# Attention with sinks, then a gated FFN on one core: scores by blocks of 128 queries in every batch, and ten uncast weight pieces instead of nine

## The chip, the core and the metric

The kernel runs on one core of one Trainium2 chip. The metric is the device time of one execution in microseconds (us), the median of several runs. The engines are called as in the profile: PE (TensorE matmul), PEld (its weight loads), DVE (VectorE), ACT (ScalarE), POOL (GpSimd) and SP (SyncE). POOL and SP issue nearly all DMAs here: POOL those that cast float32 to bfloat16 on the way, SP the uncast ones, the transposes and the stores.

## The reference

Four batches, eight heads, 768 tokens, 64 columns a head. Each query sees the first four tokens (the sinks) and the 128 tokens that end with itself. The attention's output, as 3072 tokens of 512 columns, goes through an FFN whose two halves are multiplied, and through two more matrices.

```python
keep = is_sink | in_window                       # pos < 4, or 0 <= rel < 128
a = softmax(where(keep, (q @ k.T) / 8, -1e9))    # 768 x 768 for each of 4 x 8 heads
x = (a @ v) as (3072, 512)
out = ((x @ w1) * (x @ w2)) @ w3 @ w_out         # w1, w2: 512 x 1024; w3: 1024 x 1024; w_out: 1024 x 512
```

## The kernel before

**Weights.** w3 @ w_out doesn't depend on x, so it is computed once: the *fold*. For each of the eight row blocks i of w3 (128 rows), `fold_w3` transposes its eight 128x128 pieces on PE in two groups of four ("t3", h = 0 and 1; group h needs columns 512 h to 512 h + 511) and DVE copies them to `w3t`; `fold_mm` ("fm", four pairs a row block) multiplies piece j with row block j of w_out into a PSUM tile, and ACT copies the finished row block to `w3o`. Row block i therefore needs its own row of w3 and all eight row blocks of w_out. Row blocks 0 to 3 accumulate in the ring of score tiles (`ps_sc`, two slots, two row blocks a slot), 4 to 7 in the common ring (`ps_mm`, four slots).

**How weights arrive.** `raws` lists pieces of 0.5 MB that SP loads uncast, into buffers that are needed only later (`homes`); DVE and ACT cast them (line 418, `cast`). The other rows of w3, and w1 and w2 in four column quarters ("w12"), come through POOL's queue, in the order of `order`, between the loads of q, k and v ("qkv", batch, first and last block of 128 tokens). POOL's queue begins only when the raw piece number `hold` has landed: line 204 reads one of its columns. On SP, eight small loads of the sinks' rows of v (`vc`) stand behind the pieces. The loads of batches 1 to 3 are issued when the fold is done.

**Attention.** A stage t is 256 queries, a block j is 128 queries. `transposes` (L214, then a DVE copy) or `transposes_dma` turns k and q. Then scores (PE), exp (ACT), mask (DVE), products with v (PE), reciprocal and scaling (DVE). A score tile holds 1024 columns. In stages (0, 0) and (0, 1) (`BLOCKS`) a tile is one block of 128 queries of two pairs of heads (`block_scores`, `block_values`; block 0 has no earlier keys and takes all four pairs in one tile). In all other stages a tile is one pair of heads and all 256 queries (`scores`, L261, and `values`, L351). Sink scores come from a small product (`sink_scores`), and their products with v stand in the same PSUM group as the others, one of 130 columns for a pair of heads and 128 queries. The result `xn` is transposed to `xT` on PE with an ACT copy (`block_x_transposes`, `x_transposes`, "xt") or by DMA on SP for the stages in `X_XPOSE` (`x_transposes_dma`, "xd").

**FFN.** `gate` makes x @ w1 (ACT copies it to `a_sb`) and x @ w2 (DVE multiplies) for 128 columns dt and a chunk of 256 or 384 tokens (`CHUNKS`); dt needs weight pair dt // 2. `project` multiplies with `w3o`, ACT copies and SP stores 128 tokens.

**Order.** Every step is a generator in `tasks`, with estimated stages (engine, us), what it needs, a priority and a ring. `plan` is a list scheduler: it models when loads land (`landings`, into `arrive`), takes for PE the task that can start first (by priority among those that can start at once), and emits instructions in that order, so the order on each engine is fixed when the program is built. `nudge` shifts single priorities. `PACE` sets a least distance in us between the starts of score tasks (by batch and stage), `BACKLOG` how much work ACT may have queued when one starts, `started` makes a task wait until another was placed. Where PE would idle for over 0.5 us early on, `keep_busy` puts products with zeros (L469, `pz`).

Of the kernel before, what the change touches and what calls it, by code (L numbers as in the profile page):

```python
# [21 lines left out]
def kernel(  # L22
# [13 lines left out]
    nc = tc.nc  # L36
# [92 lines left out]
    def load(what, *i):  # L129
# [9 lines left out]
        else:  # L139
            for dst, src in ((w1_sb, moe_w1), (w2_sb, moe_w2)):  # L140
# [12 lines left out]
    nudge = {("p", 3, 5, 256): -60, ("g", 1, 2, 5, 0): -300, ("tpk", 1, 5): 300, ("fm", 3, 3): 300,  # L153
             ("av", 2, 3, 2): 300}
# [8 lines left out]
    def load_raw(n, what, i0, i1, act):  # L163
        home, at = homes[n]
        tile_ = home[:, at:at + 2048].bitcast(FP32)
        nc.sync.dma_start(out=tile_.rearrange("p (k n) -> p k n", k=1), in_=fold_rows(what, i0, i1))  # L166
        return flat((w3_sb if what == "w3" else wo_sb)[:, i0:i1, :], "k n"), tile_
# [35 lines left out]
    if hold:  # L203
        nc.gpsimd.tensor_copy(spent[:], casts[hold - 1][1][:, 0:1])
# [44 lines left out]
    def segments(t):  # L249
        segs = [] if t == 0 else [(2 * t - 1, 2 * t, P, 0)]  # L250
        return segs + [(2 * t, 2 * t, 2 * P, P), (2 * t + 1, 2 * t + 1, P, 3 * P)]

    ams = {}

    def scores(b, r, t):
        c0 = P if t == 0 else 0
        sc = ps_sc.tile([P, 2, 512], FP32, tag="sc", name="sc")
        for i, (kb, qb, n, c) in enumerate(segments(t)):
            for e in range(2):
                hp = slice(64 * e, 64 * e + 64)  # L260
                nc.tensor.matmul(sc[:, e, c:c + n], kT[b][hp, r, kb * P:(kb + 1) * P],  # L261
                                 qT[b][hp, r, qb * P:qb * P + n],
                                 start=True, stop=True)
        yield
        ex = work.tile([P, 2, 512], BF16, tag="ex", name="ex")
        nc.scalar.activation(ex[:, :, c0:], sc[:, :, c0:], ACTF.Exp, scale=scale)  # L266
        yield
        am = work.tile([P, 2, 512], BF16, tag="am", bufs=4, name="am")
        mk = maskt[:, min(t, 1):min(t, 1) + 1, c0:].to_broadcast([P, 2, 512 - c0])
        nc.vector.tensor_mul(am[:, :, c0:], ex[:, :, c0:], mk)  # L270
        ams[b, r, t] = am
        yield
# [26 lines left out]
    def block_values(b, j, r0):  # L299

        t, i = j // 2, j % 2
        av = ps_mm.tile([P, 2, 2, D + 1], FP32, tag="mm", name="av")
        todo = []
        for r in range(r0, r0 + 2):
            if t > 0:
                q0 = (t - 1) * 256 + i * P
                todo.append((av[:, r - r0, :, :].rearrange("p e d -> p (e d)"), es[b][:, q0:q0 + P],
                             vs[b][:, 2 * r:2 * r + 2, :].rearrange("p e d -> p (e d)")))
            am, kbs = ams.pop((b, j, r))
            for s, kb in enumerate(kbs):  # L310
                for e in range(2):
                    todo.append((av[:, r - r0, e, :], am[:, e, s, :], vN[b][:, kb, 2 * r + e, 0:D + 1]))
        for n, (o, lhs, rhs) in enumerate(todo):
            nc.tensor.matmul(o, lhs, rhs, start=(n == 0), stop=(n == len(todo) - 1),  # L314
                             skip_group_check=True)
        yield
        rec = work.tile([P, 2, 2, 1], FP32, tag="rec", name="rec")
# [3 lines left out]
        nc.vector.tensor_mul(xns[b, t][:, i, r0:r0 + 2, :, :], av[:, :, :, 0:D],  # L321
                             rec[:].to_broadcast([P, 2, 2, D]))
        yield

    def block_x_transposes(b, j):
# [7 lines left out]
        yield  # L333

    def values(b, r, t):

        am = ams.pop((b, r, t))
        av = ps_mm.tile([P, 2, 2, D + 1], FP32, tag="mm", name="av")
        todo = []
        for i in range(2):  # L340
            if t > 0:
                q0 = (t - 1) * 256 + i * P
                todo.append((av[:, i, :, :].rearrange("p e d -> p (e d)"), es[b][:, q0:q0 + P],
                             vs[b][:, 2 * r:2 * r + 2, :].rearrange("p e d -> p (e d)")))
            for kb, c in ((2 * t + i - 1, 2 * i * P), (2 * t + i, (2 * i + 1) * P)):
                if kb >= 0:
                    for e in range(2):
                        todo.append((av[:, i, e, :], am[:, e, c:c + P],
                                     vN[b][:, kb, 2 * r + e, 0:D + 1]))
        for n, (o, lhs, rhs) in enumerate(todo):  # L350
# [5 lines left out]
        if r == 0:  # L356
            xns[b, t] = work.tile([P, 2, NP, 2, D], BF16, tag="xn", bufs=3, name="xn")
# [476 lines left out]
```

## Time and profile before

| | |
|---|---|
| median of 3 runs | 195.89 us (195.88 to 197.36) |
| profiled execution: span from first to last instruction | 194.9 us (the page gives no other time for it) |
| instructions | 4621 |
| granted TensorE clock, mean | 1.000 |
| HBM read, written | 29.39 MB, 6.29 MB |

The page gives busy time and instruction count per engine, the span in 40 slices (each digit is the busy share in tenths), the DMA queues, the chain of work that ended last, and groups of instructions. A group reads: line, engine, operation, output<-inputs, partitions x elements and type, count | busy us, mean ns of one | idle us of the engine just before, and what ended it. "L391" is line 391 of the kernel. In a timeline the columns are start us, us, engine and line, operation, count, and in brackets the idle time before with what ended it. In a table of windows the columns are the window, its length, then busy us and instruction count in brackets for each engine named, the granted clock, the DMA share and GB/s. A matmul's own duration includes the pipeline behind it; what one costs in a row of them is the distance between starts.

### The profile page before, as it was taken

The page shows a single profiled execution, that of the slowest core. Times are in us where ns is not written, and L with a number is a line of the kernel's source. Part 1 is how long each engine was busy: PE and PEld are TensorE (multiplying, and loading weights), DVE is VectorE, ACT ScalarE, POOL GpSimd, SP SyncE. Part 2 cuts the span into 40 slices and gives each one's busy share as a digit, 9 for nine tenths or more (in the row PEclk, how much of TensorE's full clock was granted, in tenths as well). Part 3 has the DMA queues.
Part 4 walks back from the last instruction along what each step waited for, and adds up shares of the span by engine and source line. Part 5 has one row for each costly group of instructions (what it writes and reads, how often), then busy time and mean ns, then how long its engine had stood idle before and what let it go on. Part 6 is the DMA issues. An engine that isn't in the chain of part 4 may idle for free.

```text
span 194.9 us, 4621 instructions
## 1 busy us (share of the span) xinstructions
PE 186.8 (96%) x1813; PEld 123.0 (63%) x1828; DVE 116.4 (60%) x279; ACT 104.3 (54%) x179; POOL 75.6 (39%) x102
## 2 busy tenths in 40 slices
PE   7689999999999999999899999999999999999994
PEld 2344566898866787788688555666566566664542
DVE  6474588855889887867667436854578544431000
ACT  3430678744765965675556647633766533332232
POOL 5199877779989853533344441000000000000000
PEclk9999999999999999999999999999999999999999
DMA  6999999999999999999999999999701440001344
GB/s 219 396 376 161 184 162 197 195 158 154 157 151 193 198 145 111 150 137 189 131 155 158 128 183 204 234 183 125 87 3 34 133 108 0 0 0 55 124 161 148
DMA packets 108021, 29.17 MB, mean 150 GB/s; under 512 B 98656, under 2 KB 103904, under 8 KB 108000
## 3 DMA queue, kind: packets, MB, share of 16 engines
q0 software_dynamic: 79520, 12.33, 93.0%
q1 hardware_dynamic: 28336, 16.49, 41.1%
q8 instruction: 14, 0.23, 0.5%
q10 hardware_dynamic: 144, 0.07, 0.1%
q14 instruction: 7, 0.06, 0.1%
HBM read 29.39 MB, written 6.29 MB: 183 GB/s over the span
## 4 chain that ended last, share of the span: by engine, by line
PE 84%; DMA 11%; SPq 2%; issue 1%; DVE 0%; ACT 0%; ACTq 0%
PE pg L391 39%; PE po L452 21%; PE av L351 6%; DMA kqT<-in_moe_w_out_dram 6%; PE sc L261 5%; DMA kqT<-qN 5%; PE pw L438 3%; PE tp L214 3%; PE ph L438 2%; SPq L166 2%; PE av L314 1%; PE sc L282 1%; PE sp L243 1%; PE tp L408 1%; PE xt L330 1%
## 5 line engine op out<-in xcount | busy, mean ns | idle before, releaser
L391 PE MATMUL pg<-xT,w_sb 128*128 128x256 bf16 (+1 forms) x640 | 90.0, 294 | 0.0
L391 PEld LDWEIGHTS <-w_sb 128*128 128x128 bf16 x640 | 60.0, 98 | 21.0 <-issue 1.0
L395 DVE TENSOR_TENSOR ab<-a_sb,pg 128x256 bf16<-128x256 f32 (+1 forms) x80 | 37.7, 472 | 28.7 <-PE pg L391 25.9
L398 ACT COPY a_sb<-pg 128x256 f32<-128x256 f32 (+1 forms) x80 | 33.3, 416 | 39.1 <-PE pg L391 22.4
L452 PE MATMUL po<-w3o,ab 128*128 128x512 bf16 (+2 forms) x198 | 43.3, 362 | 0.5
L266 ACT ACTIVATE ex<-sc 128x1024 bf16<-128x1024 f32 (+1 forms) x40 | 37.7, 962 | 4.6 <-PE sc L261 3.9
L452 PEld LDWEIGHTS <-ab 128*128 128x128 bf16 x208 | 19.1, 98 | 19.5 <-issue 0.3
L270 DVE TENSOR_TENSOR am<-ex,maskt 128x1024 bf16<-128x1024 bf16 (+1 forms) x40 | 25.5, 646 | 3.9 <-ACT ex L266 3.7
L456 ACT COPY w_sb<-po 128x512 f32<-128x512 f32 (+2 forms) x25 | 14.1, 565 | 25.6 <-PE po L452 25.5
L110 POOL DMA_DIRECT2D qN<-in_q_dram x24 | 21.5, 895 | 13.1 <-DMA vN<-in_v_dram 9.6
L110 POOL DMA_DIRECT2D vN<-in_v_dram x24 | 21.7, 906 | 10.4 <-DMA kN<-in_k_dram 8.8
L110 POOL DMA_DIRECT2D kN<-in_k_dram x24 | 21.6, 898 | 10.5 <-DMA qN<-in_q_dram 7.8
L358 DVE TENSOR_TENSOR xn<-av,rec 128x256 bf16<-128x256 f32 x40 | 17.0, 425 | 1.4
L351 PE MATMUL av<-vN,am 128*128 128x65 bf16 x296 | 16.7, 193 | 0.0
L351 PEld LDWEIGHTS <-am 128*128 128x128 bf16 x296 | 14.2, 97 | 2.3 <-DVE rec L355 0.3
L355 DVE RECIPROCAL rec<-av 128x4 f32<-128x4 f32 x40 | 7.2, 181 | 13.3 <-PE av L351 12.9
L261 PE MATMUL sc<-kqT 64*128 64x128 bf16 (+1 forms) x216 | 11.8, 238 | 0.6 <-DMA kqT<-qN 0.6
L351 PE MATMUL av<-vs,es 128*128 128x130 bf16 x56 | 11.1, 221 | 0.0
L216 DVE COPY kqT<-tp 128x1024 bf16<-128x1024 bf16 x12 | 8.3, 689 | 3.3 <-PE tp L214 3.1
L261 PEld LDWEIGHTS <-kqT 64*128 64x128 bf16 x216 | 7.0, 94 | 4.2 <-issue 3.3
L438 PE MATMUL ph<-wo_sb,w3t 128*128 128x512 bf16 x32 | 8.2, 380 | 0.8 <-DVE wo_sb L418 0.4
L286 ACT ACTIVATE ex<-sc 128x1024 bf16<-128x1024 f32 x7 | 7.2, 1032 | 2.0 <-PE sc L282 2.0
(71 smaller groups left out, 128.1 us busy)
## 6 DMA issues: line engine op xcount, KB each, us to landing
out_dram<-w_sb SPq DMA_DIRECT2D x20, 256.0 KB
kN<-in_k_dram POOLq DMA_DIRECT2D x24, 128.0 KB, 8.3
qN<-in_q_dram POOLq DMA_DIRECT2D x24, 128.0 KB, 8.1
vN<-in_v_dram POOLq DMA_DIRECT2D x24, 128.0 KB, 8.0
w_sb<-in_moe_w_dram POOLq DMA_DIRECT2D x9, 256.0 KB, 8.5
ab<-in_moe_w_dram SPq DMA_DIRECT2D x4, 512.0 KB
ab<-in_moe_w_out_dram SPq DMA_DIRECT2D x2, 512.0 KB
out_dram<-w_sb SPq DMA_DIRECT2D x7, 128.0 KB
```

The lines of the kernel that those rows point to most:

```text
L110: nc.gpsimd.dma_start(out=dst, in_=rows(src, b, kb))
L261: nc.tensor.matmul(sc[:, e, c:c + n], kT[b][hp, r, kb * P:(kb + 1) * P], qT[b][hp, r, qb * P:qb * P + n], start=True, stop=True)
L266: nc.scalar.activation(ex[:, :, c0:], sc[:, :, c0:], ACTF.Exp, scale=scale)
L270: nc.vector.tensor_mul(am[:, :, c0:], ex[:, :, c0:], mk)
L351: nc.tensor.matmul(o, lhs, rhs, start=(n == 0), stop=(n == len(todo) - 1), skip_group_check=True)
L358: nc.vector.tensor_mul(xns[b, t][:, :, r, :, :], av[:, :, :, 0:D], rec[:].to_broadcast([P, 2, 2, D]))
L391: nc.tensor.matmul(pg[:], w_sb[:, kk, dt * P:(dt + 1) * P], xT[b][:, kk, tk], start=(kk == 0), stop=(kk == NP - 1))
L395: nc.vector.tensor_mul(ab[b][:, dt, tk], gate_a.pop((b, c, dt))[:], pg[:])
L398: nc.scalar.copy(a_sb[:], pg[:])
L438: nc.tensor.matmul(po, w3T[i][:, j, :], wo_sb[:, j, :], start=(j == 0), stop=(j == KFF - 1))
L452: nc.tensor.matmul(po[:], ab[b][:, kk, m * P:(m + 1) * P], w3o[:, kk, n0:n1], start=(kk == 0), stop=(kk == KFF - 1))
L456: (nc.vector.tensor_copy if n0 == DM // 2 else nc.scalar.copy)(o_sb, po[:])
```

## The change

- **Blocks everywhere.** `scores`, `values`, `x_transposes` and `segments` go; all stages use `block_scores` and `block_values`. The two score tiles of a block are issued one right behind the other ("glue"), but for block 0 and block 1 of batch 0 (`SINGLE`). A block waits only for its own two blocks of keys.
- **Sink products** of a block's two pairs of heads become one of 260 columns instead of two of 130. (`sink_products`, `glued_values` and `glued_normalize` are added, but `GLUED` is empty, so they are never used.)
- **Stage (0, 2)** turns x by DMA instead of on PE.
- **Raw pieces.** Ten instead of nine; those of w3 are 512 columns of two row blocks instead of 1024 columns of one. w_out comes whole and w3 rows 0 to 5 as raw pieces; rows 6 and 7 through POOL (before, rows 5 to 7). Every piece is cast in two halves of 512 columns, one on DVE and one on ACT. `hold` goes from 5 to 6.
- **Order of POOL's loads**: blocks 4 and 5 of batch 0 come ahead of the last two quarters of w1 and w2.
- **Gates of batch 0** wait (`started`) only for gates of their own chunk.
- **Planning numbers**: landing times, PACE, BACKLOG 1.6 to 9.9, 35 nudges instead of five.

```diff
-    BLOCKS = ((0, 0), (0, 1))
+    GLUED = tuple((b, j) for b in range(0) for j in (2, 3, 4))
-    PAIRS = (2, 3)
-    X_XPOSE = ((1, 0), (1, 1), (1, 2), (2, 0), (2, 1), (2, 2), (3, 0), (3, 1), (3, 2))
+    SINGLE = ((0, 1),)
+    X_XPOSE = ((0, 2), (1, 0), (1, 1), (1, 2), (2, 0), (2, 1), (2, 2), (3, 0), (3, 1), (3, 2))
...
-    raws = [("w3", 4, 5, "both"), ("wo", 0, 2, "act"), ("w3", 2, 3, "both"), ("w3", 1, 2, "both"),
-            ("wo", 2, 4, "both"), ("w3", 3, 4, "both"), ("w3", 0, 1, "both"), ("wo", 6, 8, "dve"),
-            ("wo", 4, 6, "dve")]
-    hold = 5
-
-    order = [("qkv", 0, 0, 1), ("w3", 5, 6), ("qkv", 0, 1, 2), ("w3", 6, 8), ("qkv", 0, 2, 3),
-             ("qkv", 0, 3, 4), ("w12", 0, 1), ("w12", 1, 2), ("w12", 2, 3), ("w12", 3, 4), ("qkv", 0, 4, 5),
-             ("qkv", 0, 5, 6), ("qkv", 1, 0, 6), ("qkv", 2, 0, 6), ("qkv", 3, 0, 6)]
+    raws = [("w3", 2, 4, 0), ("wo", 0, 2), ("wo", 2, 4), ("w3", 0, 2, 0), ("w3", 4, 6, 0), ("w3", 2, 4, 1),
+            ("wo", 4, 6), ("w3", 0, 2, 1), ("wo", 6, 8), ("w3", 4, 6, 1)]
+    hold = 6
+
+    order = [("qkv", 0, 0, 1), ("qkv", 0, 1, 2), ("w3", 7, 8), ("qkv", 0, 2, 3), ("qkv", 0, 3, 4), ("w3", 6, 7),
+             ("w12", 0, 1), ("w12", 1, 2), ("qkv", 0, 4, 5), ("qkv", 0, 5, 6), ("w12", 2, 3), ("w12", 3, 4),
+             ("qkv", 1, 0, 2), ("qkv", 1, 2, 4), ("qkv", 1, 4, 6), ("qkv", 2, 0, 6), ("qkv", 3, 0, 6)]
...
+    def load_raw(n, what, i0, i1, *half):
...
+        if half:
+            src = src[:, :, half[0] * 512:half[0] * 512 + 512]
...
+    def block_products(b, j, r0, sinks):
...
+        if sinks:
+            q0 = (t - 1) * 256 + i * P
+            todo.append((av[:].rearrange("p r e d -> p (r e d)"), es[b][:, q0:q0 + P],
+                         vs[b][:, 2 * r0:2 * r0 + 4, :].rearrange("p h d -> p (h d)")))
         for r in range(r0, r0 + 2):
-            if t > 0:
-                q0 = (t - 1) * 256 + i * P
-                todo.append((av[:, r - r0, :, :].rearrange("p e d -> p (e d)"), es[b][:, q0:q0 + P],
-                             vs[b][:, 2 * r:2 * r + 2, :].rearrange("p e d -> p (e d)")))
...
-        queues = {"sp": [(RAW, 1.28, 1.0 if n < 2 else 1.9, [("raw",) + x[:3]]) for n, x in enumerate(raws)],
-                  "pool": [(gen, us, 1.8, keys) for x in order for gen, us, keys in service(*x)]}
+        queues = {"sp": [(RAW, 1.28, 0.55 if n < 2 else 1.35, [("raw",) + x]) for n, x in enumerate(raws)],
+                  "pool": [(gen, us, 1.45, keys) for x in order for gen, us, keys in service(*x)]}
...
+            for j in kbs:
+                halves = [(0, NP)] if j == 0 else [(0, 2), (2, NP)]
+                ready = [(n, b, kb) for kb in (j - 1, j) if kb >= 0
+                         for n in (("tdk", "tdq") if (b, kb // 2) in XPOSE else ("tpk",))]
...
+                    single = (b, j) in SINGLE or j == 0
+                    lead, more = r0 == 0 and not single, r0 > 0 and not single
...
-                     [("g",) + gates[-2] + (1,)] if len(gates) > 1 else [])
+                     [("g",) + x + (1,) for x in gates[-2:-1] if b or x[1] == c])
...
-    PACE = [[0, 3, 3], [3, 0, 3], [0, 7.4, 6.1], [0, 0, 0]]
-    TURN, SHAPE = 0.095, {"sc": 1, "ss": 2}
+    PACE = [[0, 0, 2.15], [3.8, 0.65, 0.2], [1.75, 0.65, 0.5], [2.75, 3.65, 1.75]]
+    TURN, SHAPE = 0.095, {"sc": 1, "sa": 1, "ss": 2}
...
-    BACKLOG = 1.6
+    BACKLOG = 9.9
```

More of the change, by code (lines that the diff above doesn't have):

```diff
@@ L203 @@
     if hold:
-        nc.gpsimd.tensor_copy(spent[:], casts[hold - 1][1][:, 0:1])
+        nc.gpsimd.tensor_copy(spent[:], casts[hold - 1][0][2][:, 0:1])
     for x in order:
@@ L315, in block_values, with sink_products, block_normalize @@
                              skip_group_check=True)
+    def sink_products(b, j):
+        q0 = (j - 2) * P
+        for h in range(2):
+            hp = slice(64 * h, 64 * h + 64)
+            nc.tensor.matmul(avt[b, j, 2 * h][:].rearrange("p r e d -> p (r e d)"), es[b][hp, q0:q0 + P],
+                             vs[b][hp, 4 * h:4 * h + 4, :].rearrange("p h d -> p (h d)"),
+                             start=False, stop=True, skip_group_check=True)
         yield
+    def block_normalize(b, j, r0):
+        t, i = j // 2, j % 2
+        av = avt.pop((b, j, r0))
         rec = work.tile([P, 2, 2, 1], FP32, tag="rec", name="rec")
@@ L690, in occupy, with pe_est, met @@
             rings[ring] = [c for c in rings[ring] if c is not old] + [cell]
+        def pe_est(k, ahead=()):
+            def met(a, known):
+                return a in known or a in ahead
+            if any(not met(a, begun) for a in k["started"]):
+                return None
+            if any(not met(a, begun if k["half"] else done) for a in k["after"]):
+                return None
+            est = max([free["pe"]] + [arrive[x] + HOP for x in k["loads"]])
+            if not k["half"]:
+                est = max([est] + [done[a] + HOP for a in k["after"] if a in done])
+            return est
         def pe_pick():
@@ L731, in advance @@
                 k["cell"][0] = at
[L732 to L733 removed]
+            if i == len(k["stages"]) - 1:
+                for x in k["frees"]:
+                    tasks[x]["cell"][0] = at
             k["stage"] = i + 1
@@ L771, in plan @@
                 k = pe[1]
+                forced = forced[1:] if forced else list(k["glue"])
                 gap = start - max(free["pe"], START)
```

248 lines of the change are left out of this document (97 added, 151 removed), and 8 rows, old and new, of the table nudge.

## The prediction

> **What bounds the kernel now.** I read the head of the page first: busy time per engine, then the forty slices.
>
> ```profile
> span 194.9 us, 4621 instructions
> PE 186.8 (96%) x1813; PEld 123.0 (63%) x1828; DVE 116.4 (60%) x279; ACT 104.3 (54%) x179; POOL 75.6 (39%) x102
> ...
> PE   7689999999999999999899999999999999999994
> ...
> DMA  6999999999999999999999999999701440001344
> ```
>
> PE is full from the fourth slice on, so about 15 us. The next question is whether it ever waits after that: the list of waits for PE alone from 18.2 to 192 us, then one window of PE's busy time between the last weight cast and the end of its last matmul.
>
> ```profile
> PE sc L261 <- DMA kqT<-qN: 0.6, 1, 0.6
> PE pw L438 <- issue: 0.2, 1, 0.2
> ```
>
> ```profile
> 15.76:192.02 176.26, 174.52 (x1741) 1.00 1.39 135
> ```
>
> Waits of 0.8 us in 174 us, at a clock of 1.00: behind about 16 us the kernel is a sum of PE work. Two things can move the end: less PE work behind that point, or more of it done ahead. The chain of waits shows why PE is late in front, and prices the pieces (start, us, what).
>
> ```profile
> 4.66 11.08 DMA kqT<-in_moe_w_out_dram
> 15.76 0.70 DVE wo_sb L418
> 16.50 1.89 PE ph L438 x8
> 18.39 0.45 PE tp L214 x8
> ...
> 20.56 0.22 PE tp L408 x4
> 20.79 0.33 PE sc L282 x8
> ...
> 29.13 0.55 PE sc L282 x16
> ...
> 34.56 0.87 PE pg L391 x8
> ...
> 47.54 0.55 PE sc L261 x12
> ...
> 55.90 0.22 PE xt L367 x4
> 56.13 0.44 PE sc L261 x8
> ...
> 84.61 9.42 DMA kqT<-qN
> ```
>
> The chain starts with the ninth uncast piece of weights, which lands at 15.7 us. What PE did by 18.2 us is counted by line: the fold's products (L438), its transposes (L408), and the idle products that only keep PE running (L469), in this order.
>
> ```profile
> 0.00:18.20 18.20, 7.02 (x28) 2.43 (x28) 1.00 1.14 297
> ```
>
> ```profile
> 0.00:18.20 18.20, 3.26 (x40) 2.39 (x40) 1.00 1.14 297
> ```
>
> ```profile
> 0.00:18.20 18.20, 5.63 (x15) 1.73 (x16) 1.00 1.14 297
> ```
>
> A fold product costs 0.216 us (the chain's eight are followed by a transpose that starts 1.73 us after the first), a transpose 0.055 us (four in 0.22). So 28 x 0.216 + 40 x 0.055 = 8.2 us of real work stand in the first 18.2 us; 10 us are lost there. The whole fold is 64 products and 64 transposes, 17.3 us.
>
> **Term 1: what the new pieces let PE do early.** The pieces land at a steady beat, read from the casts that wait for them (ACT, and the last one here DVE).
>
> ```profile
> 4.27 0.62 ACT L418 CAST w_sb<-ab 128x512 bf16<-128x512 f32 x1 [2.18 <-DMA ab<-in_moe_w_dram]
> ...
> 7.59 0.62 ACT L418 CAST w_sb<-ab 128x512 bf16<-128x512 f32 x1 [1.05 <-DMA ab<-in_moe_w_dram]
> ...
> 12.72 0.62 ACT L418 CAST w_sb<-kN 128x512 bf16<-128x512 f32 x1 [0.67 <-DMA kN<-in_moe_w_dram]
> ...
> 14.30 0.88 DVE L418 CAST wo_sb<-qN 128x1024 bf16<-128x1024 f32 x1
> ```
>
> Four beats from 7.59 to 12.72 make 1.28 us a piece, then 1.5 us once POOL's loads share the DMA. I keep these times for the new pieces and put the tenth at 17.2. Before, a w3 piece is one row block of 1024 columns, and half of it is useless until the late wo pieces are there. A new piece is 512 columns of two row blocks, and those need only wo blocks 0 to 3, the second and third piece. By hand: pieces 1 to 3 allow 8 products (rows 2, 3); the fourth (8.88) 8 more, the fifth (10.15) 8 more; the seventh (wo 4, 5) 4, the eighth 4, the ninth 8: 40 products by the ninth piece instead of 28. From 9.5 us on PE is never out of them: 0.45 + 0.4 (copy) + 1.73 for piece four, 0.45 + 1.73 for five, 0.45 for six, 0.86 for seven, 0.45 + 0.86 for eight, 1.73 for nine, which ends at 18.6. At 18.2 it has done 38 products: 10 x 0.216 = **2.2 us ahead**.
>
> Is there work to keep it ahead? POOL's queue is held until piece 5 before and piece 6 after.
>
> ```profile
> 10.18 0.19 POOL L204 COPY spent<-ab 128x1 f32<-128x1 f32 x1 [4.47 <-DMA ab<-in_moe_w_out_dram]
> ...
> 10.38 1.04 POOL L110 DMA_DIRECT2D kN<-in_k_dram  x1
> ...
> 24.52 0.75 POOL L113 DMA_DIRECT2D w_sb<-in_moe_w_dram  x1 [0.86 <-DMA w_sb<-in_moe_w_dram]
> ...
> 28.27 0.74 POOL L113 DMA_DIRECT2D w_sb<-in_moe_w_dram  x1 [0.16 <-issue]
> ```
>
> ```profile
> w_sb<-in_moe_w_dram POOLq DMA_DIRECT2D x1, 256.0 KB, 7.5
> ```
>
> ```profile
> w_sb<-in_moe_w_dram POOLq DMA_DIRECT2D x1, 256.0 KB, 9.2
> ```
>
> The last number of such a row is the time from issue to landing: the load issued at 24.52, the second half of the first w1/w2 pair, lands at 32.0; the one at 28.27, four loads on, at 37.5, so these loads of 0.5 MB land 1.37 us apart. The whole POOL queue moves back 1.28 us and loses one w3 row block of 0.5 MB ahead of this pair, so the pair keeps its time; k, q, v of blocks 2 and 3 come about 1 us earlier (two row blocks fewer ahead of them), and the last two weight pairs 5.4 us later (six q/k/v loads of 0.9 us pass them). Up to 29.5 us, when the last w3 row lands (two loads ahead of 32.0), PE can at most have done seven rows of fold (7 x 2.17 = 15.2) and some 6.4 us of attention (four tp 1.8, scores 2.1, the rest sinks, values and xt): 21.6 us. Before, it had done 8.2 + 11.1 - 0.2 = 19.1 by then. So 2.5 us of lead fit, in the best order; tp to copy to scores to exp to mask to values costs 3 to 4 us a block, and some holes of 0.2 to 0.5 us are sure. Behind 32 us the gates of the first two weight pairs for two chunks (16 halves of 0.435 us, 7 us; chained only within a chunk, so they needn't wait for the late pairs) and blocks 4 and 5 fill PE until the next pair lands at 37.5 + 5.4 = 43 us. I carry **1.8 us** (bounds 0 and 2.6).
>
> The piece itself could be slower: its runs are 2 KB instead of 4 KB. Nearest rows: the weight loads above, with runs of 1 KB and the same 0.5 MB read, take 1.37 us; at this beat six pieces lose 0.6 us. I take 0, since 2 KB is as near to 4 KB and the queue is the pieces' own. The Trainium skill ("DMA: Bandwidth & Descriptors", Why small descriptors are slow) has a fixed cost of about three cycles a packet, beside one per 32 bytes; by an estimate from that page a 2 KB run would cost 2% more, 0.2 us over six pieces, and the sum would be 0.2 us later. No row here shows 2 KB loads.
>
> **Term 2: PE work that goes.** Block (0, 2) turns its x by DMA: two groups of four transposes (the xt row), **0.44 us**, and two ACT copies, off the path. Its two transposes on SP are moved past nothing:
>
> ```profile
> 15.75 0.25 SPq L202 DMA_DIRECT2D vc<-in_v_dram  x1
> 56.10 7.70 SPq L461 DMA_DIRECT2D out_dram<-w_sb  x3
> ```
>
> They land at worst 9.4 us later (last row of the chain), where an xt and its copy take under 1. Sixteen gate halves of the other two chunks, 7 us, and the projections behind them cover this; uncovered, it would cost up to 8.6 us.
>
> The sink products become one of 260 columns for two of 130.
>
> ```profile
> 33.24 0.23 PE L314 MATMUL av<-vs,es 128*128 128x130 bf16 x1
> 33.31 0.29 PE L314 MATMUL av<-vN,am 128*128 128x65 bf16 x4
> 33.43 0.22 PE L314 MATMUL av<-vs,es 128*128 128x130 bf16 x1
> ```
>
> Start to start 0.06 to 0.07 each; a gate product of 256 columns takes 0.109 (0.87 / 8), so 260 columns about 0.111. 32 pairs save 0.01 each, **0.3 us** (bounds 0 and 0.6). Scores by blocks cost the same: a pair is 0.55 in sixteen products or in twelve, and t = 0 is 0.33 + 0.55 instead of 2 x 0.44. Exps and masks of t = 0 fall from four to three a batch, on engines at 54 and 60%.
>
> **Term 3: order.** New paces, nudges and expected landings reorder all of it. Nothing prices that; the present order loses only 0.8 us, so it can give 0.8 and take more. I take 0 (bounds -0.8 and +2).
>
> **Sum.** 194.9 - 1.8 - 0.44 - 0.3 = 192.4 us of span. The page gives no other time for that execution; the median of the runs is 195.89, 1.0 above the span, so **193.4 us**, 1.3% faster. A difference under 1% can't be told from none here.
>
> **Rivals.**
> 1. *The lead is eaten by the loads.* Held 1.28 us longer, POOL lets PE run dry between 20 and 33 us. DVE helps: it waits for the sink rows of v, whose small loads stand behind the pieces on SP.
>
> ```profile
> 20.49 0.69 DVE L234 TENSOR_TENSOR vs<-vc,ones_s 128x512 bf16<-128x512 f32 x1 [0.92 <-DMA vc<-in_v_dram]
> ```
>
> One more piece makes this about 1.3 us later, and the copies of block 1 and the first mask stand behind it. For it: only 2.5 us of lead fit. Against: fold rows 4, 5 and 7 fill holes. Term 2 alone is left: 194.9 - 0.74 + 1.0 = 195.2. In the first microseconds idle products take twice their later time:
>
> ```profile
> 1.33 3.47 PE L469 MATMUL pz<-ksbd 128*128 128x512 bf16 x8 [1.33 <-DVE ksbd L175]
> ```
>
> 0.43 us each against 0.216. The Trainium skill ("TensorE: Matmul & The Clock Gate", Part 1) says that PE's clock is halved after an idle window of some 3.4 us; by it a hole that long would put one window at half rate, 1.7 us, on top, and the time would be about 197. The granted clock of 1.00 in every window shows no such fall behind the start.
> 2. *ACT becomes the bound, slower than before.* The limit on ACT's backlog goes from 1.6 to 9.9 us, the paces of batch 2 from 7.4 and 6.1 us to 0.65 and 0.5 (t = 1, 2). Two exps then stand ahead of a gate's copy.
>
> ```profile
> L266 ACT ACTIVATE ex<-sc 128x1024 bf16<-128x1024 f32 x28 | 28.3, 1026 | 3.7 <-PE sc L261 3.1 <-DVE rec L355 0.5
> ```
>
> Two are 2.05 us, and four PSUM slots of 0.435 us cover 1.75: 0.3 us lost a pair, 15 pairs in batches 1 to 3: 4.5 us, 197.9. It decides from 0.17 us a pair. Against: batch 3 is unpaced already (140 to 155 us) and PE waits nowhere there.
> 3. *The pieces don't come at 1.28 us*: 0.6 us less lead, 194.0.
> 4. *Everything fits*: lead 2.6, no waits: 194.9 - 2.6 - 0.74 - 0.6 + 1.0 = 192.0.
>
> **Chances.** Forecast 0.45, rivals 0.25, 0.10, 0.10, 0.10. The forecast's own spread is 192.6 to 194.4, about three quarters of it under the 1% mark of 193.9; with all of rival 4 and less than half of 3, faster gets 0.48. Slower gets rival 2 and little else, 0.11; the rest is within 1%. The range takes in rivals 1, 3 and 4 and leaves rival 2 and better than everything out: 191.6 to 196.2.
>
> **What would show it.** Fold products by 18.2 us: about 38. PE's waits between 18 and 33 us: under 1 us for the forecast, over 2 for rival 1. First gate near 32 to 33 us, against 34.4. Gates' copies waiting behind exps, with PE idle, after 90 us: rival 2. I am wrong if the casts come later than the rows above, or if PE waits anywhere after 35 us for over 1 us.

## The result, and the profile after

The changed kernel takes **199.03 us** (median of 4 runs, 198.07 to 199.62) against 195.88 for the kernel before (195.43 to 197.36): 3.1 us or 1.6% more by the medians; the mean ratio is 1.0133, with a 95% interval of 1.0094 to 1.0171. Slower, clear of the interval though by less than 2%, and outside the range that was given. The profiled execution took 199.08 us, 1.7 more than its span; span and time stand 1.7 apart in the other runs too, so the profiled execution of the kernel before, with its span of 194.9, took about 196.6, 0.7 above the median. A run of the kernel before of 195.87 us has a span of 194.2, so the spans too are 3.1 apart; on the two profiles it is 2.4. Four single executions further down took over 1.5% more than the fastest of their kernel (203.44, 204.41, 489 and 1071 us), and the medians are without them.

The head of the changed kernel's page and three of its slice rows (PE's busy tenths, its granted clock, the DMA's busy tenths):

```profile
span 197.3 us, 4712 instructions
PE 187.1 (95%) x1864; PEld 123.8 (63%) x1864; DVE 115.1 (58%) x278; ACT 104.6 (53%) x177; POOL 74.3 (38%) x102
...
PE   6699899999999999979899999999999999999992
...
PEclk9789999999999999999999999999999999999999
DMA  5999999999999999999999999999323240000244
```

PE is as full as before, except for a slice with a 7 (84 to 89 us) and one with an 8 (94 to 99 us), and a granted clock of 0.7 and 0.8 in the second and third slice. Four windows of PE's busy time (start:end, length, busy, matmuls, granted clock, DMA share, GB/s), before and then after, say how much PE stood idle in each:

```profile
0.00:18.20 18.20, 14.53 (x83) 1.00 1.14 297
18.20:35.00 16.80, 16.43 (x207) 1.00 1.84 180
35.00:80.00 45.00, 44.84 (x556) 1.00 2.21 161
80.00:100.00 20.00, 19.36 (x236) 1.00 1.79 152
```

```profile
0.00:18.20 18.20, 14.62 (x81) 0.91 1.01 302
18.20:35.00 16.80, 15.93 (x204) 1.00 1.93 176
35.00:80.00 45.00, 44.67 (x571) 1.00 2.17 169
80.00:100.00 20.00, 18.11 (x225) 1.00 1.76 144
```

Idle time grows by 0.5 us between 18 and 35, 0.2 up to 80 and 1.25 between 80 and 100. (The profile of before lacks 14 matmul records, 4 of 32 fold products in `pw` and 10 of 208 in `po`. Up to 0.4 us of its idle time ahead of 80 us is such a gap, so the true growth is larger by that, and PE's busy time before is a little too small.) Another 0.6 us lies behind the last matmul, which starts and lasts (before, then after):

```profile
189.63 2.35 PE L452 MATMUL po<-w3o,ab 128*128 128x512 bf16 x20
```

```profile
191.68 2.13 PE L434 MATMUL po<-w3o,ab 128*128 128x512 bf16 x19
```

These groups end at 191.98 and 193.81, and the spans 2.9 and 3.5 later. This repeats: the stretch is 2.9 us in five other versions of the kernel before and 3.4 in the one with the new pieces, and 3.2 to 3.7 in all versions of the changed kernel. Its cause is open. The front, where 2.2 us were to be won, holds as much idle time as before (3.6 to 3.7 us). The casts on ACT, which start when a piece has landed, and POOL's first instructions show why:

```profile
5.63 0.62 ACT L400 CAST w_sb<-ab 128x512 bf16<-128x512 f32 x1 [3.55 <-DMA ab<-in_moe_w_dram]
6.89 0.62 ACT L400 CAST wo_sb<-ab 128x512 bf16<-128x512 f32 x1 [0.64 <-DMA ab<-in_moe_w_out_dram]
...
9.90 0.62 ACT L400 CAST w_sb<-ab 128x512 bf16<-128x512 f32 x1 [1.05 <-DMA ab<-in_moe_w_dram]
...
12.72 0.62 ACT L400 CAST w_sb<-ab 128x512 bf16<-128x512 f32 x1 [0.67 <-DMA ab<-in_moe_w_dram]
...
18.27 0.62 ACT L400 CAST w_sb<-kqT 128x512 bf16<-128x512 f32 x1 [0.99 <-DMA kqT<-in_moe_w_dram]
```

```profile
12.75 0.19 POOL L217 COPY spent<-ab 128x1 f32<-128x1 f32 x1 [7.34 <-DMA ab<-in_moe_w_dram]
...
26.18 0.74 POOL L113 DMA_DIRECT2D w_sb<-in_moe_w_dram  x1 [0.19 <-issue]
```

```profile
w_sb<-in_moe_w_dram POOLq DMA_DIRECT2D x1, 256.0 KB, 8.1
```

The first piece is cast at 5.63 us instead of 4.27, the sixth at 12.72 instead of 11.43; POOL, which waits for it, starts 2.57 us later than before (one piece more, each late), and the second half of the first w1/w2 pair lands at 26.18 + 8.1 = 34.3 us instead of 32.0. The fold's products by 18.2 us, and PE's waits over 18 to 192 us, each with count and longest:

```profile
0.00:18.20 18.20, 8.73 (x30) 3.06 (x31) 0.91 1.01 302
```

```profile
PE sc L272 <- DMA kqT<-qN: 1.2, 1, 1.2
PE sp L256 <- DMA kqT<-qN: 0.7, 1, 0.7
PE sc L272 <- DVE kqT L229: 0.6, 1, 0.6
PE sp L256 <- DVE kqT L229: 0.2, 1, 0.2
PE tp L227 <- DMA qN<-in_q_dram: 0.2, 1, 0.2
```

Thirty products, not 38. The 1.2 and the 0.7 are waits at 86.9 and 95.4 us for k and q of batch 2 transposed by DMA, behind loads that are late by then (the first load of batch 2, issued at 58.98 us, takes 7.8 and lands at 66.8; before, 57.28 + 6.5 = 63.8). So both marks that were to show the prediction wrong are there: later casts, and waits of over 1 us behind 35 us.

### The profile page after: what moved, and what is told of

Its sections match the earlier page's. It is cut to its first block, busy times and chain, and to the rows that moved or that the text cites. A ratio compares the mean times of both kernels' runs of the same rounds, so it can differ in the third digit from the quotient of the medians.

```text
span 197.3 us, 4712 instructions
## 1 busy us (share of the span) xinstructions
PE 187.1 (95%) x1864; PEld 123.8 (63%) x1864; DVE 115.1 (58%) x278; ACT 104.6 (53%) x177; POOL 74.3 (38%) x102
## 4 chain that ended last, share of the span: by engine, by line
PE 69%; DMA 21%; POOL 5%; SPq 2%; issue 1%; ACT 0%; DVE 0%; DVEq 0%
PE pg L373 37%; PE po L434 19%; DMA qN<-in_q_dram 9%; PE av L306 5%; DMA ab<-in_moe_w_dram 5%; PE sc L272 5%; DMA kqT<-qN 4%; DMA w_sb<-in_moe_w_dram 3%; POOL w_sb L113 2%; PE tp L227 1%; POOL kN L110 1%; SPq L175 1%; POOL qN L110 1%; POOL vN L110 1%; PE sp L256 1%
## 5 line engine op out<-in xcount | busy, mean ns | idle before, releaser
L276 ACT ACTIVATE ex<-sc 128x1024 bf16<-128x1024 f32 x44 | 43.6, 1024 | 6.9 <-PE sc L272 6.3
L280 DVE TENSOR_TENSOR am<-ex,maskt 128x1024 bf16<-128x1024 bf16 x44 | 29.5, 684 | 2.4 <-ACT ex L276 2.4
L327 DVE TENSOR_TENSOR xn<-av,rec 128x256 bf16<-128x256 f32 x48 | 20.4, 425 | 1.7
L306 PEld LDWEIGHTS <-am 128*128 128x128 bf16 x352 | 16.0, 98 | 3.4 <-DVE am L280 0.7
L324 DVE RECIPROCAL rec<-av 128x4 f32<-128x4 f32 x48 | 8.5, 178 | 14.9 <-PE av L306 14.6
L272 PE MATMUL sc<-kqT 64*128 64x128 bf16 x352 | 14.0, 217 | 1.8 <-DMA kqT<-qN 1.2
L272 PEld LDWEIGHTS <-kqT 64*128 64x128 bf16 x352 | 10.0, 94 | 5.8 <-issue 2.8
L420 PE MATMUL ph<-wo_sb,w3t 128*128 128x512 bf16 x32 | 9.7, 427 | 0.5 <-DVE wo_sb L400 0.4
L306 PE MATMUL av<-vs,es 128*128 128x260 bf16 x32 | 8.8, 275 | 0.0
L420 PEld LDWEIGHTS <-w3t 128*128 128x128 bf16 x48 | 4.3, 103 | 4.6 <-issue 1.6
```

The costliest lines, as they stand in the source:

```text
L272: nc.tensor.matmul(sc[:, e, r - r0, s, :], kT[b][hp, r, kb * P:(kb + 1) * P], qT[b][hp, r, j * P:(j + 1) * P], start=True, stop=True)
L276: nc.scalar.activation(ex[:], sc[:].rearrange("p e r s q -> p e (r s q)"), ACTF.Exp, scale=scale)
L280: nc.vector.tensor_mul(am[:].rearrange("p e (r x) -> p (e r) x", x=n), ex[:].rearrange("p e (r x) -> p (e r) x", x=n), maskt[:, v:v + 1, c ...
L420: nc.tensor.matmul(po, w3T[i][:, j, :], wo_sb[:, j, :], start=(j == 0), stop=(j == KFF - 1))
```

## The experiments

Each line gives the median, the difference from the median of the kernel before on the same chip, and the interval of the ratio. Wherever a kernel's layout is "new", the planner wrote another order of instructions; where it is "kept", the instructions of PE, DVE and POOL stand in the order of the kernel it comes from.

### The pieces

**The old front under the new blocks** (new layout).

```diff
-    raws = [("w3", 2, 4, 0), ("wo", 0, 2), ("wo", 2, 4), ...]   # ten pieces
-    hold = 6
+    raws = [("w3", 4, 5), ("wo", 0, 2), ("w3", 2, 3), ...]      # the nine of before, and its load order
+    hold = 5
```

> The changed kernel, with the nine weight pieces of before (4 KB runs), POOL held until the fifth and POOL's old order; everything else as changed. Theory A (the new pieces are the loss: their 2 KB runs come slowly, the first is cast at 5.63 us instead of 4.27, PE idles 1.75 us, its clock falls and fold products cost 0.36 to 0.38 us instead of 0.216): casts from 4.3 us on, granted clock 1.00 from 5 us on, PE idle before 40 us like before, time 196 to 197, 2 to 3 us less than the changed kernel. Rival B (the new order behind 40 us is the loss, with the stalls of PE at 85 to 95 us): still 198.5 to 199.5.

202.48 us, +6.2 (1.0287 to 1.0369). The casts fall on the times of before, and up to 35 us PE is as full as before; then it is not:

```profile
18.20:35.00 16.80, 16.59 (x206) 1.00 1.83 180
35.00:80.00 45.00, 42.67 (x547) 1.00 2.27 163
80.00:100.00 20.00, 18.59 (x221) 1.00 1.78 140
```

So undoing the pieces repairs the front and leaves PE idle for 3.7 us between 35 and 100 (2.2 in the changed kernel, 0.8 in the one before). Rival B had the place, but the time lies far above both theories; it is the first sign that the order counts for more than either.

**The new front under the old blocks** (new layout): the same edit the other way in the kernel before.

> The kernel before, with the ten new pieces, POOL held until the sixth and POOL's new order; scores, paces and the rest as before. Theory A: first cast at 5.6 us, the granted clock below 1 between 5 and 15 us, time 197.5 to 199. Rival B: 195 to 196.5, since its order behind 40 us is the old one.

201.35 us, +5.1 (1.0235 to 1.0324). The first cast is at 5.48 us here too, so the late front belongs to the pieces. The time lies above both theories, and the waits on PE are others (2.0 us on DVE's copies of the fold, 1.0 us on ACT's a_sb).

**Two queues** (layout kept): every second piece issued by ACT.

```diff
-        nc.sync.dma_start(out=tile_...
+        (nc.scalar if n % 2 else nc.sync).dma_start(out=tile_...
```

> The changed kernel, but every second uncast piece is issued by ACT instead of SP. Theory D (descriptors of one issuing queue come at some 110 to 140 a microsecond, so pieces in 2 KB runs are limited by that): the first piece still at 5.6 us, but the later ones catch up, the last cast near 17 us instead of 18.3, 0.5 to 1.5 us faster. Rival (the DMA engines or HBM are slow with 2 KB runs, or the descriptors of both queues come from one place): cast times as in the changed kernel within 0.3 us, time 198.5 to 199.5.

198.69 us, +2.4 (1.0082 to 1.0217): no better than the changed kernel beyond the intervals. The tenth cast comes at 17.55 instead of 18.27 and the ninth at 16.59 instead of 16.66, but the first at 7.05, since ACT loads its table behind its issues (at 5.76 us, for 1.28). That speaks against a limit of one queue. The Trainium skill ("DMA: Bandwidth & Descriptors", Issuing engines are not separate DMA queues) says that a second issuing engine saves only issue time; this run agrees.

**2 KB runs alone** (layout kept): in the kernel before, wo is read in two runs of 2 KB a partition instead of one of 4 KB.

```diff
-        return src.rearrange("(g ki ko) n -> ki g (ko n)", ki=P, ko=2)
+        return src.rearrange("(ko ki) n -> ki ko n", ki=P)
```

> The kernel before with nothing changed but the runs in which the four pieces of wo are read: two of 2 KB a partition instead of one of 4 KB (the order of the contraction follows). It measures what 2 KB runs cost by themselves. Theory D' (2 KB runs are slower while the queue starts, whatever the queue): the first w3 piece is cast at 4.27 us as before, the wo piece behind it 0.3 to 0.6 us later than before's 5.5, and the last pieces 0.5 to 1 us later; the loads of POOL move by as much or less, and the time by 0.5 to 1.2 us. Rival (the run's length is not the cause; the ten pieces are late because each is of two row blocks or because of their order): casts within 0.2 us of before's, time within 0.4 us.

196.71 us, +0.9 by the medians, and no difference by the interval (0.9992 to 1.0059). The casts, first, second and seventh:

```profile
4.34 0.62 ACT L418 CAST w_sb<-ab 128x512 bf16<-128x512 f32 x1 [2.25 <-DMA ab<-in_moe_w_dram]
5.77 1.04 ACT L418 CAST wo_sb<-ab 128x1024 bf16<-128x1024 f32 x1 [0.81 <-DMA ab<-in_moe_w_out_dram]
...
13.22 0.62 ACT L418 CAST w_sb<-kN 128x512 bf16<-128x512 f32 x1 [0.68 <-DMA kN<-in_moe_w_dram]
```

Late by 0.07, 0.28 and 0.50 us, about as theory D' has it. Runs of 2 KB cost something, but less than half of what the new front shows (1.36 and 1.40 us at its first two casts).

**wo first** (new layout, but nearly the order of the changed kernel): its first two pieces exchanged.

```diff
-    raws = [("w3", 2, 4, 0), ("wo", 0, 2), ("wo", 2, 4), ...
+    raws = [("wo", 0, 2), ("w3", 2, 4, 0), ("wo", 2, 4), ...
```

> The changed kernel with its first two pieces in the other order: wo 0 and 1 (runs of 4 KB) ahead of the first half of w3 rows 2 and 3 (runs of 2 KB). Theory D'' (2 KB runs are slow only while the queue starts): the wo piece is cast at 4.1 to 4.4 us, the w3 piece at 5.6 to 5.9 (both 6.89 and 5.63 in the changed kernel), the later pieces and POOL's start 0.8 to 1.2 us earlier than in the changed kernel, and the time 1 us shorter, about 198. Rival (half rows are slow wherever they stand): the second cast stays at 6.5 to 6.9 us and POOL starts within 0.3 us of the changed kernel's 12.75.

199.72 us, +3.3 (1.0063 to 1.0223). Between the two theories:

```profile
4.17 0.62 ACT L400 CAST wo_sb<-ab 128x512 bf16<-128x512 f32 x1 [2.08 <-DMA ab<-in_moe_w_out_dram]
6.91 0.62 ACT L400 CAST w_sb<-ab 128x512 bf16<-128x512 f32 x1 [2.12 <-DMA ab<-in_moe_w_dram]
```

```profile
3.00:3.50 0.50, 0.50 (x3) 0.21 (x2) 0.47 (x3) 0.00 (x0) 0.50 (x2) 1.00 1.02 406
...
4.50:5.00 0.50, 0.50 (x2) 0.15 (x1) 0.10 (x1) 0.29 (x1) 0.38 (x2) 1.00 0.74 209
5.00:5.50 0.50, 0.42 (x2) 0.00 (x0) 0.00 (x0) 0.00 (x0) 0.49 (x4) 1.00 0.82 225
```

The last number is GB/s: the wo piece (4 KB runs) comes at 406 while the queue starts, and the half rows of w3 behind it at 209 to 225. The changed kernel, where that piece is the first:

```profile
2.50:3.00 0.50, 0.50 (x2) 0.15 (x1) 0.48 (x2) 0.00 (x0) 0.44 (x1) 1.00 0.82 238
3.00:3.50 0.50, 0.50 (x3) 0.21 (x2) 0.47 (x3) 0.00 (x0) 0.50 (x2) 1.00 0.80 217
```

The later half-row pieces take 1.28 (11.44 to 12.72) to 1.67 us (8.23 to 9.90) there. So the first half-row piece costs some 1.4 us whether it stands first or second. It is short of packets (one run each): 170 of 2 KB start between 2.5 and 4.0 us in the changed kernel, 113 a microsecond, and some 150 between 4.0 and 5.5 us here, 100 a microsecond. That is about as many as while the 4 KB runs of wo come (some 100 between 2.5 and 3.5 us here), and later half rows reach 190 (285 between 8.0 and 9.5 us in the changed kernel). Why it is so for the first one alone is left open. POOL's start moves only from 12.75 to 12.28.

### The loads

**POOL later, nothing else** (layout kept): the kernel before, POOL held until the sixth piece.

```diff
-        nc.gpsimd.tensor_copy(spent[:], casts[hold - 1][1][:, 0:1])
+        nc.gpsimd.tensor_copy(spent[:], casts[hold][1][:, 0:1])
```

> The kernel before in its own order; only POOL's first loads wait for the sixth uncast piece instead of the fifth, 1.28 us later. It prices late loads in the old order, whose landing times were laid out 1 to 1.5 us later than they come. Theory E: it has that much slack, 195.9 to 196.8. Rival F: each late load costs in full, 197.2 to 197.8.

197.82 us, **+2.0** (1.0066 to 1.0132). POOL's first load is issued 1.47 us later (11.85 for 10.38), and the second half of the first w1/w2 pair lands at 26.89 + 7.5 = 34.4 us, as late as in the changed kernel:

```profile
11.85 1.04 POOL L110 DMA_DIRECT2D kN<-in_k_dram  x1
...
26.89 0.75 POOL L113 DMA_DIRECT2D w_sb<-in_moe_w_dram  x1 [1.56 <-DMA w_sb<-in_moe_w_dram]
```

```profile
PE tp L408 <- DMA w_sb<-in_moe_w_dram: 0.7, 2, 0.5
PE tp L214 <- DMA qN<-in_q_dram: 0.6, 2, 0.4
```

(The 7.5 is the row of that issue, of the same words as the prediction's.) At one and the same order, this lateness of the loads costs 2.0 us, as rival F has it. There is no slack behind 18 us to take it up.

**POOL earlier** (layout kept): the changed kernel, POOL held until the fifth piece.

> The changed kernel in the same order; only POOL's first loads wait for the fifth uncast piece instead of the sixth. Theory F: every load of POOL lands 1.0 to 1.3 us earlier, the waits of PE for copies and loads between 18 and 40 us go, time 197.5 to 198.3. Rival (the pieces are slowed by as much as POOL gains, or the loss lies behind 50 us): 198.7 to 199.4.

199.28 us, +3.5 (1.0081 to 1.0248): nothing won, as the rival has it. POOL starts 1.97 us earlier, but v's sink rows, which stand on SP, are used 0.4 us later (23.74 for 23.35). DVE waits longer for them, and PE for DVE (1.3 us, 0.6 in the changed kernel) and for the DMA transposes (2.3 us, 1.9 in the changed kernel). That POOL's loads take the DMA time of the sink rows would fit, but isn't shown.

```profile
23.74 0.69 DVE L247 TENSOR_TENSOR vs<-vc,ones_s 128x512 bf16<-128x512 f32 x1 [2.23 <-DMA vc<-in_v_dram]
```

**v's sink rows issued by ACT** (layout kept), to take them off SP's queue.

```diff
-        nc.sync.dma_start(out=vc[r0:r0 + 4, :, :], ...
+        nc.scalar.dma_start(out=vc[r0:r0 + 4, :, :], ...
```

> The changed kernel in the same order; only the eight small loads of the sinks' rows of v are issued by ACT instead of standing behind the pieces on SP. Theory H (DVE's wait of 1.57 us at 23 us holds up the copy of block 1 and the first mask, and PE with them): that wait is gone, PE idles under 0.4 us between 20 and 35 us, 0.5 to 1 us faster than the changed kernel. Rival: PE has enough else to do, under 0.3 us.

200.44 us, +4.6 (1.0193 to 1.03). It tells little on the sink rows, because the edit has a price of its own: ACT is held by its eight issues for 6.19 us, and casts nothing until 9.03. DVE's wait for the rows is gone, and PE, late from the front on, idles 0.79 us between 18 and 35 us (0.87 in the changed kernel).

```profile
2.79 6.19 ACTq L215 DMA_DIRECT2D vc<-in_v_dram  x8
9.03 0.62 ACT L400 CAST w_sb<-ab 128x512 bf16<-128x512 f32 x1 [6.94 <-DMA vc<-in_v_dram]
```

**x of block (0, 2) on PE again** (new layout).

```diff
-    X_XPOSE = ((0, 2), (1, 0), ...
+    X_XPOSE = ((1, 0), ...
```

> The changed kernel, but x of stage (0, 2) is turned on PE as before (two transposes fewer on SP). Theory C (these two DMA transposes at 47 to 55 us slow POOL's loads of batch 1, all later loads and transposes come some 2 us later, and PE stalls 1.9 us at 85 to 95 us): POOL's loads of batch 1 are issued by 56 us instead of 58, PE idles under 1 us between 80 and 100 us, time 198 or less. Rival: the stalls have to do with the order on SP and not with the two transposes: the stalls stay, PE has 0.45 us more work, time 199.0 to 199.6.

198.55 us, +2.3 (1.0082 to 1.0174). PE's idle time between 80 and 100 falls from 1.89 to 0.83 us:

```profile
80.00:100.00 20.00, 19.17 (x225) 1.00 1.72 153
```

POOL issues its last load of batch 1 at 56.86 us instead of 58.05, so theory C has the direction, though not the 2 us. But PE's idle time between 18 and 35 us grows from 0.87 to 1.96. What is left is 0.5 us less in the median, which the intervals don't separate from nothing. This run's PE had a clock of 1.00 throughout the front and had done at least 31 fold products by 18.2 us, against 30.

### The order

The planner lays the order out for landings of loads that it estimates. Compared with the profiles, the loads of batches 0 and 1 and of the weights come 0.2 to 2.3 us (mostly 1.0 to 2.3) *earlier* than planned in the kernel before and 1.1 to 3.4 us *later* than planned in the changed one. Four kernels put measured landings in the plan's place (15 to 22 lines of this kind), and nothing else changes in the kernel that is named:

```diff
     landings()
+    arrive["vc",] = 23.5
+    for raw, us in zip(raws, (5.2, 6.4, 7.7, ...)):
+        arrive[("raw",) + raw] = us
+    ...                                  # every load of POOL likewise
     plan(True)
```

**The changed kernel, true landings:**

> The changed kernel, ordered anew with the landing times that its own trace shows (first piece 5.4 us instead of 4.1, q of block 0 20.2 instead of 18.3, first w1/w2 pair 34.2 instead of 32.1, sinks of v 23.1 instead of 20.0, and so on). Theory E (its order is laid out for loads that land 2 us earlier than they do, so PE and DVE stand behind steps whose data isn't there): PE's idle time between 18 and 50 us falls below 0.6 us, time 196.5 to 198. Rival F (the loads themselves are late, and no order helps): 198.5 to 199.5. Rival G (nudges and paces fit only the order they were found with): above 199.5.

197.95 us, +2.2 (1.0049 to 1.0165). About 1 us better than the changed kernel by the medians, though the intervals overlap. The waits near 90 us are gone, but theory E's sign isn't there: PE's idle time between 18 and 50 us is 1.5 us, not below 0.6 (1.1 in the changed kernel).

**The old front under the new blocks, true landings:**

> The changed kernel with the nine pieces, hold and load order of the kernel before, and its order of instructions laid out anew for landings of loads as measured in the run of after_old_pieces. Theory E (what made that run 202.5 us was an order laid out for loads that came 1 to 4 us earlier, and the new blocks, sinks and x of (0, 2) themselves cost nothing): the losses between 50 and 115 us go, and it takes 195 to 196.5 us, level with the kernel before or a little faster. Rival G (the new form of the blocks costs the time whatever the order): still 199 us or more, with PE's waits on kqT and qN between 50 and 115 us as they were.

198.55 us, +2.8 (0.9997 to 1.0206, unclear). Worse than theory E said by 2 us, better than the same front and blocks in the first layout by 3.4, each taken against the kernel before on its own chip.

**POOL earlier, true landings:**

> The changed kernel with POOL's queue held until the fifth piece and not the sixth, and its order laid out anew for the landings measured in the run of after_pool_early (sink rows of v at 23.5 us). Theory E together with F (late loads cost their lateness, and an order laid out for other landings costs about 1 us): 196.5 to 197.3 us, about 1 us better than after_true_landings, whose loads come about 1.5 us later. Rival: the sink rows of v, which land later when POOL starts earlier, hold DVE up by the same 1 to 2 us, and the time stays at 198 us.

199.13 us, +3.3 (1.0039 to 1.0218): the theory misses again, and the new order changes nothing against 199.28.

**The kernel before, true landings** is the control: nothing changes but the order.

> The kernel before, with its order of instructions laid out anew for the landings measured in its own profile (they are 1 to 2 us earlier than its plan takes); pieces, loads, blocks and nudges stay. It prices a new layout by itself. Theory H (an order counts by how it was fitted, and any new layout of the same work loses 1 to 3 us): 197 to 199 us. Rival (a plan with true landings is at least as good as one with wrong ones): 195 to 196 us; then what after_old_pieces_true lost is the form of the blocks.

199.13 us, **+2.7** (1.0039 to 1.0179). Its windows:

```profile
0.00:18.20 18.20, 13.44 (x86) 1.00 1.14 296
18.20:35.00 16.80, 15.01 (x174) 1.00 1.82 178
35.00:80.00 45.00, 44.39 (x562) 1.00 2.14 161
```

Against the first windows above, 1.1 us are lost in the front, 1.4 up to 35 us and 0.45 up to 80, by the order alone; 0.6 are won back between 80 and 100.

**Without nudges.** The priorities set by hand for single tasks are emptied (`nudge = {}`), 5 in the kernel before and 36 in the changed one (not 34, as the expectation has it, or 35, as the list of the change has it).

> The kernel before with its five nudges of priority taken out, so the order is the plan's own. Theory H: 197 to 199 us, with new waits of PE of 1 us or more in all. Rival: the nudges move little, within 0.5 us of 195.9.

195.94 us, -0.5 (0.9928 to 1.0009): no difference, as the rival has it. On PE this order differs from that of before in a few places only (steps between 21 and 30, 62 and 77, and 119 and 122 us), so an order that is a little different can cost nothing.

> The changed kernel with its 34 nudges taken out. If they were fitted to the real times, it gets slower by 1 to 3 us (200 to 202); if they were fitted to planned landings that come 2 us late, they are worth nothing on the chip and it stays at 198 to 200 us.

201.21 us, +4.8 (1.0117 to 1.0297): about 2 us more than the changed kernel by the medians, though the intervals overlap. By that its nudges are worth something on the chip.

**The margins crossed.** Either a plan must take its loads for later than they are (M), or any layout other than the one kept loses (H). The changed kernel gets the measured landings plus the margins of the kernel before; the kernel before gets landings too early, like the changed one; and the old front under the new blocks gets the figures of the kernel before.

> The changed kernel, laid out for the measured landings of its loads plus the margins that the kernel before has (1.3 to 2.3 us for the loads of batches 0 and 1 and the weights). Theory M (a layout for loads later than they come keeps PE fed, one for loads earlier than they come lets it wait): 196 to 197 us, 2 us or more better than the changed kernel, and no wait of PE on a load. Theory H (any layout but the fitted one loses 1 to 3 us, margin or not): 198 to 200 us.

200.9 us, +4.5 (1.0177 to 1.0326): slower than both theories say.

> The kernel before, laid out for loads that come 1.2 to 3 us earlier than measured, as the layout of the changed kernel is; loads, pieces and blocks stay. Theory M: worse than before_true (199.1), 199.5 to 201 us, with waits of PE on loads of 2 us or more. Theory H: 197 to 199.5 us, no worse than before_true. If it stays at 196 us, the layout's landings are not the cause of anything.

200.02 us, +3.6 (1.0138 to 1.0206): in M's range, though PE's waits on loads come to 1.3 us and not 2.

> The changed kernel with the nine pieces, hold and load order of the kernel before and, as expected landings, the very figures that the kernel before is laid out for. Theory M and no cost of the new blocks: 195 to 196 us, as good as the kernel before or 0.7 us better. Theory H: 197 to 200 us. It is also the version that could beat both kernels.

201.46 us, +5.1 (1.0211 to 1.0324): slower than both theories say, with one wait of 2.8 us (sp on kqT).

M falls: for the kernel before, less margin is worse (195.9, 199.1, 200.0), but for the changed kernel early, true and late landings give 199.0, 197.95 and 200.9. H holds in part: the kernel before loses nothing without its nudges, the changed kernel's layout for true landings is no worse than its own, and other losses are larger than H said. What stands is the spread: with blocks, pieces and loads all fixed, the layouts of the kernel before run from 195.9 to 200.0 us, those of the changed kernel from 197.95 to 201.2, and those of the new blocks under the old front from 198.55 to 202.5. The order alone moves each of the three by 3 to 4 us (2.6 to 3.6 when each run is taken against the kernel before on its own chip). None of the versions is faster than the kernel before.

## Why the prediction was wrong

**Term 1 failed at its first step**, "I keep these times for the new pieces". The casts came later than the rows: by 1.36 us at the first, 0.64 at the third (8.23 for 7.59), 1.29 at the sixth, 1.1 at the tenth (18.27 for 17.2). The bound for it, 0.6 us from the 1 KB rows, was spread over six pieces; here more than twice as much is there at the first half-row piece, which no row of before could show. Ten products ahead became two (30 for 28, 0.4 us), and the first gate starts at 34.16 us, not at 32 to 33. Rival 3 had the right place, but took the lead alone to suffer.

**The loads are the part of Term 1 whose sign was wrong.** "The whole POOL queue moves back 1.28 us ... so the pair keeps its time" became 2.57 us and a pair 2.3 us late. A like lateness alone, in the kernel before, costs 2.0 us. The DVE wait of rival 1 grew from 0.92 to 1.57 us in the place it named, though vs came 2.9 us later (23.35 for 20.49) and not "about 1.3"; but rival 1 stopped at losing the lead; it had no price for falling behind.

**Term 2 held in the main.** The transposes of x on PE are 16 instead of 24, and a 260-column sink product holds PE for 0.11 us, as taken:

```profile
84.76 0.27 PE L306 MATMUL av<-vs,es 128*128 128x260 bf16 x1
84.87 0.41 PE L306 MATMUL av<-vN,am 128*128 128x65 bf16 x8
```

The 0.3 us for them was too much: from start to start, the 64 products of 130 columns take 3.7 us in the trace of before and the 32 of 260 columns 3.6 us in that of the changed kernel, so 0.1 to 0.2 us is saved, and 0.6 by all of Term 2. "Its two transposes on SP are moved past nothing" may be wrong: they join a queue whose later transposes of k and q PE waits for near 90 us, and with x back on PE the idle time there was halved; but that run has another order too, and idles more ahead of 35 us.

**Term 3 was put at nothing without a price:** "I take 0 (bounds -0.8 and +2)". The control shows 2.7 us for a new order of the same work, and the layouts lie 3 to 4 us apart. With 0.4 won in front, 0.6 of PE work saved and 3.1 lost, about 4.1 us are to be explained: 0.6 behind the last matmul, 2.0 for the loads' lateness, at the price that the kernel before pays for it, and 1.5 left, which the order would explain. The waits of 1.9 us at 86.9 and 95.4 us have this size, but that they are the order's is not shown: they are waits for DMA, and in the run with v's sink rows on ACT, where PE keeps the order and is late from the front on, 0.2 us of them is left. The parts don't add strictly either, as an order is laid out for its loads, and no run here has the changed kernel with the loads of before and an order as good as that of before. So how the 4.1 divide, and with it the size of Term 3 in this change, stays open. (The 1.0 us between span and median was two things, 1.7 behind the span less 0.7 by which the profiled execution lay above the median; it stands on both sides and moves the forecast by nothing.)

**The rivals.** ACT as the bound (rival 2) came nearest in time and is not what happened: PE never waits for a_sb in the changed kernel. That its 197.9 lies so near is luck. The clock did fall, though after a shorter hole than in rival 1's aside. PE waits 1.75 us for the first piece, and later runs at half rate:

```profile
7.00:8.00 1.00, 0.62 (x2) 0.76 1.03 404
8.00:9.00 1.00, 1.00 (x4) 0.50 1.06 391
9.00:10.00 1.00, 1.00 (x4) 0.50 1.04 375
10.00:11.00 1.00, 1.00 (x3) 0.53 1.05 322
```

By these rows PE runs at 0.5 for 0.48 + 1 + 1 + 0.94 = 3.4 us. That is the length of the window that the Trainium skill gives ("TensorE: Matmul & The Clock Gate", Part 1); the idle stretch ahead of it is only half as long as the idle window that the Trainium skill names. The fall isn't shown to cost anything here: PE lacks pieces in that stretch anyway, another run of the changed kernel at a mean clock of 1.000 took 199.62 us, and x of (0, 2) on PE, with 1.00 in the same windows, had only one or two products more by 18.2.

## What to carry to other kernels

Where an order is laid out by hand or by a planner and the bounding engine is 99% busy, the order is a term of the sum with the size that the control gives it (here up to 3 or 4 us of 196), not a zero with a margin: first lay out the unchanged kernel anew and see how much that alone moves. A change that wins less than this (here 0.6 us of work) can't be judged from one layout. And a gate such as "POOL waits for piece six" turns a late first piece into late loads everywhere: when a piece changes form, follow what its landing releases.

## What the runs showed of the hardware

- The first piece of half rows of w3 (runs of 2 KB) comes at 209 to 238 GB/s in the windows above, first or second in the queue, while 4 KB runs of wo come at 406 as the first piece; both are 100 to 113 packets a microsecond. Later half rows reach 190 packets a microsecond, and such pieces take 1.28 to 1.67 us. With wo in runs of 2 KB the casts are 0.5 us late by the seventh, two such pieces among them.
- Eight small loads issued by ACT held it for 6.19 us; it is an engine with work of its own, and its issues stand in that work's queue.
